# Two mixer layers move from the Gelu activation to a GELU built from Tanh, with a new plan for the schedule

## The chip, the cores and the metric

The kernel runs on one core of a Trainium2 chip. The metric is the device time of one execution in microseconds (us). Six runs of the kernel before lie between 1075.77 and 1081.0 us, with a median of 1077.77 us. In this text PE is the matrix engine (TensorE), ACT the activation engine (ScalarE), DVE the vector engine (VectorE), POOL is GpSimd and SP is the engine that issues most DMAs.

## What is computed

Two layers, each an attention block and a mixer block, on x of shape 1 x 2048 x 448 in bf16. Cut to what matters:

```python
def _A_ref(x, wqkv, wo):            # attention, 16 heads of 28
    q, k, v = split(x @ wqkv)
    p = softmax(q @ k.T * 28 ** -0.5)
    return (p @ v) @ wo
def _B_ref(x, w1, w2, w3, w4):      # mixer, F = 1792
    h = gelu_tanh(layernorm(x) @ w1)
    hs = shift_quarters_by(-1, +1, -2, +2)(h) @ w2
    x1 = x + hs
    return x1 + gelu_tanh(layernorm(x1) @ w3) @ w4
for _ in range(2):
    x = x + _A_ref(layernorm(x), wqkv, wo)
    x = x + _B_ref(layernorm(x), w1, w2, w3, w4)
```

The GELU is the one with tanh: gelu(x) = x/2 * (1 + tanh(sqrt(2/pi) * (x + 0.044715 x^3))). "The wide GELU" below is the one of the last line, on 1792 features of a token.

## The kernel before

**Tiles and work.** The 2048 tokens are 16 tiles of 128. Attention goes over query chunks of each layer: tiles 0-3, 4-7, 8-11, 12-13 and 14-15. For a chunk and a group of four heads (a "segment") the scores of one key tile and one head are a block of 128 keys x 512 (chunk and keys so arranged that a block is always 512 wide); there are 1024 blocks per layer. PE makes the scores (line 1292), ACT takes the exponential of three or two blocks at a time out of PSUM into the tile `PT` (line 1447), and PE multiplies with v (line 753). A few blocks do not go to ACT: the planner may give a block to DVE, which computes its exponential in five instructions (lines 1333, 1354, 1356, 1358, 1361, through the tiles `yd`, `fb` and `PD`). How many of a segment may go that way is bounded by the table `D_RATE` for (layer, chunk); a further condition is that the plan shows PE idle there and that buffers are free.

**The mixer.** When a chunk's attention is done, the output projection (lines 762, 1606) and the first mixer half `t_mixA` follow. Its GELU is already built from Tanh (`t_tanh`): DVE halves the matmul's result into `hT` (line 1676), POOL squares it into a buffer of `fb` (1694), DVE does one scalar_tensor_tensor (1695), ACT the Tanh in place (1696), DVE a second scalar_tensor_tensor (1697). `fb` has three buffers of 512 floats a partition; the DVE exponentials and the attention's normalisation (line 1548) take buffers from the same three.

The second half `t_mixB` works on groups of tiles 0-2, 3-6, 7-10, 11-12 and 13-15 of each layer. A group's 14 products with `w3`, each 128 features x 256, 384 or 512 tokens, are cast by DVE from PSUM to the bf16 tile `h2T` (line 1813, operation CAST). When all 14 are there, ACT applies one `Gelu_apprx_tanh` over all of them in place (line 1822: 128 x 7168 for four tiles, 5376 for three, 3584 for two), and PE multiplies with `w4` (line 762, `ps<-w,h2T`). Work after the last exponential does it directly from PSUM (line 1809, and lines with PT or vaug as output). Exponential and Tanh use one activation table, this Gelu another, so that a Gelu between exponentials brings two ACT_TABLE_LOADs, one ahead of it (listed under line 1822) and one ahead of the next exponential (line 1447).

**What sets the order.** Nothing is issued dynamically. When the program is built, a list scheduler (`Sched`) runs generators, one per piece of work, against durations written in the code, and fixes the order of the instructions on each engine; at run time each engine goes through its own list in order and waits on semaphores. If two pieces are ready at once, the lower rank goes first. Ranks come from `RANK` (a and b: the two mixer halves of a chunk, k and q: projections of keys and queries), `Q_LEAD` says how many segments ahead the queries of a chunk are loaded, `PE_NORM` where the normalisation is done by PE. On ACT the instruction that is ready first goes first. PE keeps two PSUM banks for everything but scores and the product with v (`misc`); it fills planned gaps with matmuls on `ident` (line 1863), which compute nothing that is used.

Of the kernel before, what the change touches and what calls it, by code (L numbers as in the profile page):

```python
# [513 lines left out]
DLO = 5  # L514
DHI = 7
DPK = 2
RANK = {k: round(1.1 + 0.05 * i, 3) for i, k in enumerate([('b', 0, 0), ('a', 0, 0), ('k', 0, 1), ('b', 0, 1), ('k', 0, 2), ('k', 1, 0), ('q', 0, 2), ('q', 0, 1), ('k', 1, 2), ('a', 0, 1), ('k', 1, 1), ('q', 0, 3), ('q', 1, 0), ('b', 0, 3), ('k', 0, 3), ('q', 1, 1), ('a', 0, 2), ('b', 0, 4), ('b', 0, 2), ('a', 0, 3), ('a', 0, 4), ('k', 1, 4), ('b', 1, 0), ('a', 1, 0), ('a', 1, 3), ('k', 1, 3), ('a', 1, 4), ('a', 1, 2), ('a', 1, 1), ('b', 1, 4), ('q', 1, 2), ('b', 1, 3), ('q', 1, 3), ('b', 1, 2), ('b', 1, 1)])}
Q_LEAD = {(0, 1): 6, (0, 2): 9, (0, 3): 3, (1, 0): 7, (1, 1): 9, (1, 2): 4, (1, 3): 5}
D_RATE = {(0, 0): 0.08, (0, 1): 0.05, (0, 2): 0.05, (0, 3): 0.06, (1, 0): 0.16, (1, 1): 0.1, (1, 2): 0.16}
PE_NORM = {(0, 0): False, (0, 1): False, (0, 2): False, (0, 3): False, (0, 4): False, (1, 0): False, (1, 1): False, (1, 2): False, (1, 3): False, (1, 4): True}  # L520
Sched.AGED = 0.1
Sched.TARGET = 0.64
Sched.LOW = 0
# [21 lines left out]
def build_kernel(nc, A_x, A_wqkv, A_wo, B_x, B_w1, B_w2, B_w3, B_w4, out, n_layers=2):  # L545
# [78 lines left out]
    with st:  # L624
# [97 lines left out]
        def num1(r):  # L722
            return int(r[1:])
# [4 lines left out]
        def op(eng, dur, fn, reads=(), writes=(), **kw):  # L728
            return (eng, dur, fn, list(reads), list(writes), kw)
# [36 lines left out]
        def later(ops, bank=None, sigs=()):  # L766
            for o in ops:
                yield o
            if bank is not None:
                yield ("rel", bank)  # L770
            for g_ in sigs:
                yield ("sig", g_)
# [913 lines left out]
                if t % HR == 0 and t > 0:  # L1686
                    yield ("spawn", t_halo(L, t), 2)

        def t_tanh(L, t0, grp, z, NW, hk):
            yield ("wait", ("hz", L, t0, grp))  # L1690
            fr = yield ("acq", FB, hk)
            fk = ("fb", num1(fr))
            f = fb[0:112, num1(fr), 0:NW]
            yield op("pool", 0.2 + NW * 0.00165, lambda e: e.tensor_tensor(out=f, in0=z, in1=z, op=ALU.mult), reads=hk, writes=[fk])  # L1694
            yield op("dve", 0.05 + NW * 0.00108, lambda e: e.scalar_tensor_tensor(out=f, in0=f, scalar=0.25 / GK, in1=z, op0=ALU.add, op1=ALU.mult), reads=hk + [fk], writes=[fk])
            yield op("act", c_act(NW), lambda e: e.activation(out=f, in_=f, func=ACT.Tanh, scale=8.0 * GK * (2.0 / math.pi) ** 0.5), reads=[fk], writes=[fk], tab="exp")  # L1696
            yield op("dve", 0.05 + NW * 0.00108, lambda e: e.scalar_tensor_tensor(out=z, in0=f, scalar=1.0, in1=z, op0=ALU.add, op1=ALU.mult), reads=hk + [fk], writes=hk)
            yield ("rel", fr)
            yield ("sig", ("hA", L, t0, grp))

        def t_halo(L, t):
            yield ("wait", ("mixA", L, t - 1))
# [69 lines left out]
        def t_mixB(L, tiles, direct, pr):  # L1772
# [25 lines left out]
            else:  # L1798
                yield ("acq", [hname], [("xT", xt)])
                hb, hkey = h2T, [[("h2T", f), ("xst",)] for f in range(14)]  # L1800
            late = []
            for fch in range(14):
                b = yield misc(("xT", xt))
                for fc in FCS:
                    yield op("pe", c_mm(NW), (mm4 if NW > 300 else mm)(ps[:, bi(b), 0:NW], w3[:, fc, 128 * fch:128 * fch + 128], xv(xt)[:, fc, 0:NW], fc == 0, fc == 3),
                             reads=[("xT", xt), ("w3",)], writes=[("ps", bi(b))], touch=[b], mode="col4" if NW > 300 else "plain")
                hk = hkey[fch]
                if direct or ("tail",) in SC.events:
                    ev = op("act", c_act(NW), lambda e, fch=fch, b=b: e.activation(out=hb[:, fch, 0:NW], in_=ps[:, bi(b), 0:NW], func=ACT.Gelu_apprx_tanh),
                             reads=[("ps", bi(b))], writes=hk, touch=[b], tab="gelu")  # L1810
                else:
                    late.append(fch)
                    ev = op("dve", c_ps(NW), lambda e, fch=fch, b=b: e.tensor_copy(out=hb[:, fch, 0:NW], in_=ps[:, bi(b), 0:NW]),  # L1813
                            reads=[("ps", bi(b))], writes=hk, touch=[b])
                yield ("spawn", later([ev], b, [("h2", L, tiles[0], fch)]), 1.5)
            yield ("rel", x_)
            for fch in range(14) if not direct else ():
                yield ("wait", ("h2", L, tiles[0], fch))
            if late:
                nl = len(late)  # L1820
# [3 lines left out]
            for i, t in enumerate(tiles):  # L1824
# [2 lines left out]
                b = yield misc(hkey[late[-1] if late else 0][0])  # L1827
                yield ("wait", ("xx1", L, t))
                for fch in range(14):
                    if direct:  # L1830
                        yield ("wait", ("h2", L, tiles[0], fch))
                    yield op("pe", c_mm(D) + 0.0, mm4(ps[:, bi(b), 0:D], hb[:, fch, 128 * i:128 * i + 128], w4[:, fch, :], fch == 0, fch == 13),
                             reads=[hkey[fch][0], ("w4",)], writes=[("ps", bi(b))], touch=[b], mode="col4", slack=slack if fch == 0 else 0.0)
                if L == 0:
# [126 lines left out]
```

## Time and profile before

| what | value |
|---|---|
| median of six runs | 1077.77 us |
| the execution that was profiled | 1080.7 us |
| its span, first to last instruction | 1079.0 us |
| granted TensorE clock, mean | 0.992 |
| ACT exponentials (line 1447) | 805, busy 921.9 us |
| blocks exponentiated on DVE (line 1333) | 37 |
| wide Gelus in one piece (line 1822) | 8, busy with their table loads 41.9 + 10.3 us |
| Tanh instructions (line 1696) | 36 |
| table loads | 16: one at the start, 8 ahead of a Gelu, 7 ahead of an exponential |
| last exponential's successor starts at | 1024.54 us |

The eight wide Gelus start, in us of the span, at 236.48, 376.69, 520.32, 609.20 and 653.92 (layer one) and at 840.95, 915.26 and 1025.83 (layer two). Their widths name the tile groups: the one at 609.20 is the only 3584-wide one, tiles 11-12 of layer one; the one at 915.26 is 7168 wide, tiles 3-6 of layer two. The page gives busy time as a union, so that instructions which overlap on one engine count once; the mean duration of one instruction includes the overlap with its neighbour.

### The profile page before, as it was taken

How to read it: one execution, taken by the hardware profiler on the slowest of the kernel's cores; microseconds unless marked ns; L12 is line 12 of the kernel's file. 1: busy time of each engine (PE TensorE's matmuls, PEld its weight loads, DVE VectorE, ACT ScalarE, POOL GpSimd, SP SyncE). 2: the span in 40 equal slices, each digit the busy share in tenths (PEclk: the TensorE clock that was granted, in tenths of full speed). 3: DMA queues.
4: the chain of work that ended last, by engine and by line, in shares of the span. 5: the costliest groups of instructions: out<-in, count | busy, mean ns of one | idle time of the engine just before them, and what ended most of it. 6: DMA issues, size and time to landing. Idle time of an engine off the chain costs nothing.

```text
span 1079.0 us, 35127 instructions
## 1 busy us (share of the span) xinstructions
PE 1009.4 (94%) x15921; PEld 421.1 (39%) x15921; DVE 637.2 (59%) x1234; ACT 1018.0 (94%) x919; POOL 313.1 (29%) x506
## 2 busy tenths in 40 slices
PE   6999999999999999899999999999989999999998
PEld 2333443443333344344433333353333433443465
DVE  8777669946569525766256553524796394554551
ACT  6898999999999999999999999999999999999951
POOL 2244124401254014452042201102743030432130
PEclk9999999999999999999999999999999999999999
DMA  4647221003111022120121133413411110220000
GB/s 114 138 112 211 76 56 32 23 17 91 32 32 32 12 69 66 44 42 20 38 81 45 26 97 98 132 53 105 84 27 27 42 40 12 53 58 16 12 11 32
DMA packets 92613, 62.24 MB, mean 58 GB/s; under 512 B 64688, under 2 KB 82368, under 8 KB 92464
## 3 DMA queue, kind: packets, MB, share of 16 engines
q1 hardware_dynamic: 89088, 51.92, 18.6%
q0 software_dynamic: 3376, 8.09, 2.7%
q8 instruction: 124, 2.03, 0.8%
q14 instruction: 25, 0.20, 0.1%
HBM read 27.12 MB, written 15.71 MB: 40 GB/s over the span
## 4 chain that ended last, share of the span: by engine, by line
ACT 70%; PE 18%; DVE 7%; DMA 2%; issue 1%; SPq 1%; POOL 1%; DVEq 0%
ACT PT L1447 63%; PE ps L762 10%; PE ps L1292 4%; ACT h2T L1822 4%; PE ps L753 3%; ACT fb L1696 1%; ACT L1822 1%; DVE fb L1356 1%; PE ps L1863 1%; DMA rT<-ub 1%; DVE PD L1361 1%; ACT L1447 1%; DVE rT L1541 1%; DVE yd L1333 1%; DVE fb L1354 1%
## 5 line engine op out<-in xcount | busy, mean ns | idle before, releaser
L1447 ACT ACTIVATE PT<-ps 128x1536 bf16<-128x1536 f32 (+1 forms) x805 | 921.9, 1335 | 20.0 <-PE ps L1292 19.2
L1292 PE MATMUL ps<-qT,kT 32*128 32x512 bf16 (+1 forms) x2560 | 315.6, 341 | 31.7 <-ACT PT L1447 23.4
L753 PE MATMUL ps<-PT,vaug 128*32 128x512 bf16 (+1 forms) x2523 | 252.3, 342 | 0.0
L1292 PEld LDWEIGHTS ps<-qT,kT 32*128 32x128 bf16 x2560 | 80.7, 91 | 309.2 <-ACT PT L1447 278.7
L1863 PE MATMUL ps<-ident 128*32 128x256 bf16 x3688 | 166.1, 275 | 3.7 <-POOL ident L842 1.5
L762 PE MATMUL ps<-xT,w 128*32 128x512 bf16 (+2 forms) x1600 | 127.7, 360 | 2.8 <-DVE h2T L1813 1.9
L1863 PEld LDWEIGHTS ps<-ident 128*32 128x32 bf16 x3688 | 105.2, 97 | 31.6 <-issue 12.1
L1813 DVE CAST h2T<-ps 128x512 bf16<-128x512 f32 (+2 forms) x112 | 67.9, 606 | 80.5 <-PE ps L762 73.1
L762 PE MATMUL ps<-w,h2T 128*32 128x448 bf16 x1512 | 104.8, 365 | 10.2 <-ACT h2T L1822 9.8
L753 PEld LDWEIGHTS ps<-PT,vaug 128*32 128x32 bf16 x2523 | 74.6, 95 | 94.9 <-issue 81.6
L1552 POOL TENSOR_TENSOR otn<-ub,fb 128x512 bf16<-128x512 f32 (+1 forms) x36 | 40.4, 1121 | 174.5 <-DMA fb<-rscr 174.5
L1088 POOL TENSOR_TENSOR sq<-kT 128x512 bf16<-128x512 bf16 (+2 forms) x32 | 30.0, 941 | 121.2 <-DVE kT L1102 120.6
L1694 POOL TENSOR_TENSOR fb<-hT 112x512 f32<-112x512 bf16 (+1 forms) x36 | 37.7, 1049 | 82.9 <-DVE hT L1676 73.5
L762 PEld LDWEIGHTS ps<-w,h2T 128*32 128x32 bf16 x1512 | 42.2, 98 | 47.0 <-issue 18.2
L762 PEld LDWEIGHTS ps<-xT,w 128*32 128x32 bf16 (+1 forms) x1600 | 44.1, 95 | 42.0 <-issue 19.3
L1768 POOL TENSOR_TENSOR x_res<-x_res,x1b 128x448 f32<-128x448 f32 x32 | 40.3, 1263 | 23.9 <-DVE xn L959 23.8
L1333 DVE TENSOR_SCALAR yd<-ps 128x512 int32<-128x512 f32 x37 | 24.9, 679 | 34.4 <-PE ps L1292 34.1
L1541 DVE RECIPROCAL rT<-rT 16x128 f32<-16x128 f32 (+1 forms) x36 | 33.5, 932 | 17.9 <-DMA rT<-ub 17.9
L1822 ACT ACTIVATE h2T<-h2T 128x7168 bf16<-128x7168 bf16 (+2 forms) x8 | 41.9, 5244 | 0.1
L762 PE MATMUL ps<-kT,w 128*32 128x512 bf16 (+1 forms) x576 | 40.1, 360 | 1.9 <-DVE qT L1164 1.1
L1526 DVE COPY ub<-ps 128x512 f32<-128x512 f32 (+1 forms) x40 | 23.3, 583 | 30.7 <-PE ps L753 30.1
L762 PE MATMUL ps<-xT,wq_pad 128*32 128x512 bf16 x448 | 41.0, 405 | 0.3 <-DVE qT L1135 0.2
(164 smaller groups left out, 1168.4 us busy)
## 6 DMA issues: line engine op xcount, KB each, us to landing
uscr<-ub SPq DMA_DIRECT2D x24, 256.0 KB, 2.0
ub<-uscr SPq DMA_DIRECT2D x24, 256.0 KB
fb<-rscr SPq DMA_DIRECT2D x24, 256.0 KB
xnd<-xn SPq DMA_DIRECT2D x28, 128.0 KB, 2.0
x_res<-in_A_x_dram POOLq DMA_DIRECT2D x16, 224.0 KB, 4.2
xd<-x_res SPq DMA_DIRECT2D x16, 224.0 KB, 2.2
x_res<-xd SPq DMA_DIRECT2D x16, 224.0 KB, 4.2
out_dram<-obf SPq DMA_DIRECT2D x16, 112.0 KB
```

The lines of the kernel that those rows point to most:

```text
L753: return lambda e: e.matmul(out=out, lhsT=lhsT, rhs=rhs, start=start, stop=stop, **kw)
L762: r.append(e.matmul(out=out[c:c + w, :], lhsT=lhsT[:, c:c + w], rhs=rhs, start=start, stop=stop, tile_position=(0, c)))
L1292: yield op("pe", max(0.055, 0.22 / nc_ * NW / 512.0), lambda e, i=i, kc=kc, j=j, g=g, a=a, NW=NW, bank=bank: e.matmul(out=ps[:, bank, i * ...
L1333: yield op("dve", c_ps(512), lambda e: e.tensor_scalar(out=y, in0=ps[:, bi(bank), :], scalar1=SCALE * L2E * FS, scalar2=-126.0 * FS, op0=A ...
L1447: yield op("act", 0.06 + n * w * 0.000833, lambda e, bk=bk, s0=s0, n=n, w=w: e.activation(out=PT[:, s0:s0 + n, 0:w], in_=ps[:, bk[0]:bk[0] ...
L1541: yield op("dve", 0.86, lambda e: e.reciprocal(out=rT[0:4 * n, :], in_=rT[0:4 * n, :]), reads=[("rT",)], writes=[("rT",)])
L1552: yield op("pool", 0.2 + NW * 0.0021, lambda e: e.tensor_tensor(out=otn[:, g, 0:NW], in0=u, in1=rb[:, 0:NW], op=ALU.mult), reads=[uk, fk], ...
L1694: yield op("pool", 0.2 + NW * 0.00165, lambda e: e.tensor_tensor(out=f, in0=z, in1=z, op=ALU.mult), reads=hk, writes=[fk])
L1768: yield op("pool", 1.2, lambda e: e.tensor_tensor(out=X, in0=X, in1=X1, op=ALU.add), reads=[xk, ("x1b", s)], writes=[xk], deps=[nop_])
L1813: ev = op("dve", c_ps(NW), lambda e, fch=fch, b=b: e.tensor_copy(out=hb[:, fch, 0:NW], in_=ps[:, bi(b), 0:NW]), reads=[("ps", bi(b))], wri ...
L1822: yield op("act", c_act(nl * NW), lambda e: e.activation(out=hb[:, 0:nl, 0:NW], in_=hb[:, 0:nl, 0:NW], func=ACT.Gelu_apprx_tanh), reads=al ...
L1863: return [e.matmul(out=ps[32 * c:32 * c + 32, bi(b), 0:256].rearrange("p (a n) -> p a n", n=128), lhsT=ident[:, 32 * c:32 * c + 32], rhs=i ...
```

## The change

The tile groups 11-12 of layer one and 3-6 of layer two no longer use the one Gelu. For them the step from PSUM to `h2T` multiplies by 0.5, and a new generator does the five-step GELU of `t_tanh` in place on 512 columns at a time: one of the 14 feature blocks for four tiles, two of them for two tiles. That makes 14 pieces for tiles 3-6 and 7 for tiles 11-12. The matmuls with `w4` wait for each feature block's piece instead of for the one Gelu. `t_tanh` itself is only rewritten to use the shared function. `RANK`, `Q_LEAD` and `D_RATE` get new values (22 of the 35 keys of RANK change their place, by one to five places; the queries of tiles 8-11 of layer two rise by four; D_RATE of layer two falls from 0.16 to 0.03 for tiles 0-3 and from 0.16 to 0.1 for tiles 8-11).

```diff
-RANK = {... [('b',0,0),('a',0,0),('k',0,1),('b',0,1),('k',0,2),('k',1,0),('q',0,2),('q',0,1),('k',1,2),... ('k',1,4),('b',1,0),('a',1,0),('a',1,3),('k',1,3),('a',1,4),('a',1,2),('a',1,1),('b',1,4),('q',1,2),('b',1,3),('q',1,3),('b',1,2),('b',1,1)]}
-Q_LEAD = {(0, 1): 6, (0, 2): 9, (0, 3): 3, (1, 0): 7, (1, 1): 9, (1, 2): 4, (1, 3): 5}
-D_RATE = {(0, 0): 0.08, (0, 1): 0.05, (0, 2): 0.05, (0, 3): 0.06, (1, 0): 0.16, (1, 1): 0.1, (1, 2): 0.16}
+RANK = {... [('a',0,0),('b',0,0),('k',0,1),('k',0,2),('k',1,0),('k',1,2),('q',0,2),('b',0,1),('q',0,1),... ('b',0,2),('a',1,0),('a',1,3),('a',1,2),('q',1,2),('k',1,3),('a',1,4),('a',1,1),('b',1,4),('b',1,3),('q',1,3),('b',1,2),('b',1,1)]}
+Q_LEAD = {(0, 1): 4, (0, 2): 9, (0, 3): 3, (1, 0): 7, (1, 1): 10, (1, 2): 4, (1, 3): 5}
+D_RATE = {(0, 0): 0.08, (0, 1): 0.05, (0, 2): 0.05, (0, 3): 0.06, (1, 0): 0.03, (1, 1): 0.1, (1, 2): 0.1}
+TANHW = {(0, 0): 0, (0, 3): 0, (0, 7): 0, (0, 11): 1, (0, 13): 0, (1, 0): 0, (1, 3): 1, (1, 7): 0, (1, 11): 0}
...
+        def tanh_gelu(z, rows, NW, hk, view):
             fr = yield ("acq", FB, hk)
             fk = ("fb", num1(fr))
+            f = view(fb[0:rows, num1(fr), 0:NW])
             yield op("pool", ..., lambda e: e.tensor_tensor(out=f, in0=z, in1=z, op=ALU.mult), ...)
             yield op("dve", ..., lambda e: e.scalar_tensor_tensor(out=f, in0=f, scalar=0.25 / GK, in1=z, op0=ALU.add, op1=ALU.mult), ...)
             yield op("act", ..., lambda e: e.activation(out=f, in_=f, func=ACT.Tanh, scale=8.0 * GK * (2.0 / math.pi) ** 0.5), ..., tab="exp")
             yield op("dve", ..., lambda e: e.scalar_tensor_tensor(out=z, in0=f, scalar=1.0, in1=z, op0=ALU.add, op1=ALU.mult), ...)
             yield ("rel", fr)
+        def t_tanh_w(L, t0, fs, hb, NW, hk):
+            for fch in fs:
+                yield ("wait", ("h2", L, t0, fch))
+            z = hb[:, fs[0]:fs[-1] + 1, 0:NW]
+            yield from tanh_gelu(z, 128, NW * len(fs), hk, lambda f: f.rearrange("p (a n) -> p a n", n=NW))
+            for fch in fs:
+                yield ("sig", ("h2g", L, t0, fch))
...
+            soft = TANHW.get((L, tiles[0]), 0) and not direct
+            fps = 512 // NW
...
+                if soft:
+                    ev = op("dve", c_ps(NW), lambda e, fch=fch, b=b: e.tensor_scalar(out=hb[:, fch, 0:NW], in0=ps[:, bi(b), 0:NW], scalar1=0.5, scalar2=None, op0=ALU.mult), ...)
+                elif direct or ("tail",) in SC.events:
...
+                if soft and (fch % fps == fps - 1 or fch == 13):
...
+                    yield ("spawn", t_tanh_w(L, tiles[0], fs, hb, NW, hks), pr)
...
-            for fch in range(14) if not direct else ():
+            for fch in range(14) if not direct and not soft else ():
                 yield ("wait", ("h2", L, tiles[0], fch))
...
-                    if direct:
-                        yield ("wait", ("h2", L, tiles[0], fch))
+                    if direct or soft:
+                        yield ("wait", ("h2g" if soft else "h2", L, tiles[0], fch))
```

## Prediction

> **What bounds the kernel now.** I read the busy shares first, then the chain of work that ended last, then the activation groups with shapes kept apart, the waits, and last the two places where the Gelus stand in the timeline. The page, in order: busy time of ACT, the 40 slices of ACT, the chain by engine.
>
> ```profile
> PE 1009.4 (94%) x15921; PEld 421.1 (39%) x15921; DVE 637.2 (59%) x1234; ACT 1018.0 (94%) x919; POOL 313.1 (29%) x506
> ...
> ACT  6898999999999999999999999999999999999951
> ...
> ACT 70%; PE 18%; DVE 7%; DMA 2%; issue 1%; SPq 1%; POOL 1%; DVEq 0%
> ```
>
> ACT is full from the third slice to the 38th; only the last 50 us (slices 39 and 40) have it idle. PE's 94% is less than it seems, since 166 us of it are the filler matmuls of line 1863. ACT waits little: in the waits of ACT the exponentials stand still 19.2 us in 15 places, nearly always for scores:
>
> ```profile
> ACT PT L1447 <- PE ps L1292: 19.2, 15, 4.0
> ```
>
> In the timeline 9.4 us of these fall before 88 us (1.89, 3.96, 3.58); the rest are a dozen of 0.3 to 2.4 us. So up to the last exponential (1024.5 us) the time is the sum of what ACT does plus those stalls, and a microsecond taken from ACT there is worth one. After it come 54.5 us in which PE has matmuls back to back; ACT is no bound there.
>
> The two Gelus that the change touches, as ACT's timeline shows them (start, duration):
>
> ```profile
> 606.87 1.02 ACT L1447 ACTIVATE PT<-ps 128x1024 bf16<-128x1024 f32 x1
> 607.90 1.28 ACT L1822 ACT_TABLE_LOAD   x1
> 609.20 3.19 ACT L1822 ACTIVATE h2T<-h2T 128x3584 bf16<-128x3584 bf16 x1
> 612.40 1.28 ACT L1447 ACT_TABLE_LOAD   x1
> 613.70 1.45 ACT L1447 ACTIVATE PT<-ps 128x1536 bf16<-128x1536 f32 x1
> ```
>
> ```profile
> 913.97 1.28 ACT L1822 ACT_TABLE_LOAD   x1
> 915.26 6.18 ACT L1822 ACTIVATE h2T<-h2T 128x7168 bf16<-128x7168 bf16 x1
> 921.46 1.28 ACT L1447 ACT_TABLE_LOAD   x1
> 922.75 2.37 ACT L1447 ACTIVATE PT<-ps 128x1024 bf16<-128x1024 f32 x2
> ```
>
> And two Tanhs of the first mixer half between exponentials: no table load, and the next instruction starts 0.52 us after the Tanh, though its own duration reads 0.63 to 0.67.
>
> ```profile
> 776.63 0.63 ACT L1696 ACTIVATE fb<-fb 112x512 f32<-112x512 f32 x1
> 777.15 4.62 ACT L1447 ACTIVATE PT<-ps 128x1536 bf16<-128x1536 f32 x4
> 781.62 0.67 ACT L1696 ACTIVATE fb<-fb 112x512 f32<-112x512 f32 x1
> 782.14 1.49 ACT L1447 ACTIVATE PT<-ps 128x1536 bf16<-128x1536 f32 x1
> ```
>
> **ACT, removed.** From the first load to the next exponential: 613.70 - 607.90 = 5.80 us and 922.75 - 913.97 = 8.78 us, together 14.58. Ahead of a load the exponential before must drain. The groups of line 1447 sum to 622.0 + 452.2 + 0.8 = 1075.0 us against 921.9 busy, so neighbours overlap by 153.1 / 805 = 0.19 us, lost once at each place: 0.38. Removed: 14.96 us.
>
> **ACT, added.** 14 pieces for tiles 3-6 and 7 for tiles 11-12, each 512 columns. The rows above give 0.52 us each in line (112 or 128 partitions are worked in parallel): 21 x 0.52 = 10.92. If every one stood alone it would be the mean duration of the 512-wide form, 0.71: 14.9. Net: 14.96 - 10.92 = **-4.0 us** (0.0 if all stand alone).
>
> [...]
>
> **DVE and POOL, added.** The cast becomes a scaling with the same shapes: 0.689 (line 1813) against 0.685 us (line 1676), nothing. Each piece adds two scalar_tensor_tensors (lines 1695 and 1697: median 0.68, mean 0.83) and one POOL multiply (median 1.04). For tiles 11-12 that is 14 x 0.68 = 9.5 us of DVE and 7.3 of POOL around 590 to 612, where DVE is 6 to 7 tenths busy: hidden. For tiles 3-6 it is 28 x 0.68 = 19.0 us of DVE and 14.6 of POOL. There DVE, in stretches of 10 us, reads:
>
> ```profile
> 860.00:870.00 10.00, 6.56 (x13) 1.00 0.19 49
> 870.00:880.00 10.00, 9.70 (x16) 1.00 0.21 43
> 880.00:890.00 10.00, 9.86 (x17) 1.00 0.08 28
> 890.00:900.00 10.00, 5.96 (x10) 1.00 0.01 2
> 900.00:910.00 10.00, 3.97 (x6) 1.00 0.08 29
> 910.00:920.00 10.00, 6.09 (x13) 1.00 0.02 5
> ```
>
> The sum is 42.1 of 60 us, idle 17.9: the added 19.0 fill it, at the mean of 0.83 (23.2) overfill it by 5.4. The casts lie at 883 to 913, so most of the pieces fall in the later, emptier rows and can run past 920. I count it as hidden; what it costs uncovered is the slow rival.
>
> Latency: the first Tanh of the run starts on POOL at 183.1 and its second scalar_tensor_tensor ends at 188.1, so a piece needs 5.0 us and holds one of three `fb` buffers: 14 pieces need at least 14 / 3 x 5.0 = 23.3 us, less than the 29 us in which the casts come. The last piece ends 5.0 us after the last cast (912.7), so `w4` can start near 917.7 instead of 921.5; nothing on the path gains by it directly. The wait on each piece stands on PE ahead of the `w4` matmuls; scores queue behind it in PE's order. And the first `w4` product may take one of two free PSUM banks a few us before the last piece is done. Planned right this costs nothing; the case that it isn't is in the rivals.
>
> GpSimd's multiply meets DVE's two-input instructions: in the trace a scalar_tensor_tensor of line 1356 lasts 1.52 us at 877.99 beside a POOL add from 877.43 to 878.95, against its median of 0.685. [...]
>
> **DVE exponentials.** A block on DVE takes 921.9 / 2011 = 0.458 us from ACT (2011 = 3 x 402 + 2 x 402 + 1 blocks on ACT) and costs DVE 0.68 + 0.76 + 0.83 + 0.44 + 0.71 = 3.4 us. Of the 37, ten lie in layer two's tiles 8-11 (785 to 887 us), five of them in the segment from 869 on; one lies at 616.6 in its tiles 0-3. With 0.03 that last chunk still allows 0.03 x 4 x 7 = 0.84, so one a segment: nothing need go. With 0.1 the sixth key block allows 2.4 where 0.16 allowed 3.84, so three taken instead of four. I take two blocks lost: **+0.9 us**. Bounds: three gained elsewhere (-1.4), all ten lost (+4.6).
>
> **The new order.** No row shows it. The stall it most plainly touches is that of ACT at 743.84 (2.37 us) and its echo at 772.01 (0.85): a query projection of layer two was evacuated late, because DVE's list had a reciprocal ahead of it that waited 3.21 us for a DMA (at 739.59). The queries of tiles 8-11 rise four ranks. Both stalls gone is -3.2; a like pair new is +3.2. I take **-1.0**, nearer to nothing. The stalls before 88 us hang on the first key and value projections, whose ranks among each other hardly change: 0.
>
> **The tail.** Tiles 7-10's last cast (1023.12) ends just before the last exponential. Were it earlier, their Gelu would go among the exponentials: 6.18 + 2 x 1.28 + 0.19 = 8.9 us more for ACT, against 10.9 us of `w4` matmuls (224) taken out of the tail: -2.0. Were the casts to stay where they are while ACT ends 4 us sooner, ACT would wait, but those matmuls are PE's last work (from 1065), 33 us after the Gelu's end, so it is covered; +2.6 without that cover. I take 0.
>
> **Sum.** -4.0 + 0.9 - 1.0 + 0 = -4.1 us: 1080.7 - 4.1 = 1076.6 for the profiled execution. That one was 2.9 us above the median of six, so on the median 1077.77 - 4.1 = **1073.7 us**.
>
> **Rivals.**
> *More is gained* (0.25): the seam stalls go, no DVE block is lost, the tail swap comes: -4.0 - 3.2 - 2.0 = -9.2, 1068.6. For it: ACT is the bound everywhere and every term is there in the rows; against it, they must all fall right.
> *Nothing is left* (0.10): the change does remove four loads but its room on DVE is paid with five DVE blocks (+2.3) and one stall of about 1: -0.7, 1077.1. For it: D_RATE falls just where the pieces go.
> *Slower* (0.23): DVE becomes the bound around tiles 3-6. Already before, the chain runs through DVE from 870.85 to 886.8 and ACT loses 0.68 there. With 5.4 us of excess passed on to the scores through late casts and query evacuations, and one more seam like 743.84: -4.0 + 0.9 + 5.4 + 2.4 = +4.7, 1082.4. It decides from the point where ACT stands still 7.2 us longer than before. Against it: DVE is 59% busy over the span, and DVE blocks can give way.
> *The forecast* (0.42): 1072 to 1075.5.
>
> **Numbers.** A measurement of this kernel can tell about 0.3%, 3.2 us, from no change: below 1074.5 counts as faster, above 1081.0 as slower. Of the forecast 0.32 lies below 1074.5 and 0.10 above. Faster: 0.32 + 0.25 = 0.57. Same: 0.10 + 0.10 = 0.20. Slower: 0.23. The range takes in most of both rivals, 1068 to 1083, and leaves about 0.1 out on each side.
>
> **What would show it.** Right: 12 table loads instead of 16, six wide Gelus, 57 Tanhs, ACT's busy time some 3 us less, 35 or so DVE blocks, the last exponential done about 4 us sooner with a tail still near 54 us. Wrong: ACT's wait for scores well above 19.2 us, above all after 860 us; DVE full for 30 us on end there; far fewer than 35 blocks; or a tail of other length, which would mean that the order, not the tables, made the difference.

## The result, and the profile after

The kernel after the change takes 1084.16 us in the median of its 16 timed runs, the kernel before 1078.12 us (37 runs): a ratio of **1.0055, 95% interval 1.0043 to 1.0067**. The change makes the kernel slower by 6 us where 4 us less were forecast. The execution that was profiled took 1084.23 us, with a span of 1082.5 us and a mean granted TensorE clock of 0.992.

Lines of the kernel after are those of before plus one from line 753 on (1292 becomes 1293, 1447 becomes 1448), the Gelu is line 1845, the cast 1830, the new scaling 1823, the fillers 1886; 1694 to 1697 (the pieces of the Tanh GELU) keep their numbers.

The page of the kernel after: busy time by engine, then ACT's 40 slices.

```profile
PE 1002.3 (93%) x15701; PEld 414.8 (38%) x15701; DVE 664.4 (61%) x1273; ACT 1015.6 (94%) x937; POOL 345.1 (32%) x527
...
ACT  6898999999999999999999999999998989999952
```

ACT does 2.4 us less than before and the span is still 3.5 us longer. The new thing is in the slices: an 8 stands at 31 and at 33, where before there were nines from the fifth slice to the 38th. A slice is 27 us, so the place is 812 to 893 us. The waits of ACT (engine, line, what it waited for; total, times, longest) tell the same:

```profile
ACT PT L1448 <- PE ps L1293: 21.0, 20, 4.0
...
ACT fb L1696 <- DVE fb L1695: 3.4, 3, 1.5
```

The exponentials wait 1.8 us longer than before, and Tanhs now make ACT wait 3.4 us, before 0.1: ACT takes its list in order, so a Tanh whose DVE step is late holds up the exponentials behind it (1.52 us at 887.37, below).

What the tables promised is there: 12 table loads, 6 wide Gelus, 57 Tanhs. All 37 DVE blocks are still there. To see where the time went I cut the stream of exponentials at the same number of finished blocks in both traces, and split ACT's time of each stage (from the start of one instruction to the start of the next, in us, idle time apart):

| blocks done | before: length, idle | after: length, idle | difference |
|---|---|---|---|
| 0 to 1000 | 512.0, 20.4 | 508.5, 17.5 | -3.5 |
| 1000 to 1250 (tiles 11-12 of layer one) | 131.3, 1.2 | 128.6, 0.8 | -2.7 |
| 1250 to 1500 | 123.2, 2.4 | 122.3, 1.6 | -0.9 |
| 1500 to 1750 (766 to 895 us) | 127.9, 2.4 | 135.7, 8.8 | +7.8 |
| 1750 to 1875 (tiles 3-6 of layer two) | 67.2, 0.1 | 70.2, 3.9 | +3.0 |
| 1875 to 2011 | 62.9, 0.0 | 62.8, 0.1 | -0.2 |
| tail after the last exponential | 54.45 | 54.43 | 0.0 |

So the change is 7 us ahead at 760 us and has lost 10.8 us by 965. Of the 7 the 2.7 of tiles 11-12 are its own. The 3.5 of the first 1000 blocks, where only the order differs, are mostly chance of one execution: the profiled run of before had four stretches of half clock before 530 us (see the last section), that of after none, and three kernels below that have the tables of before (e1, e1b, v4) need 509.1 to 510.3 us for these blocks. Over the whole stream Gelus lose 9.4, table loads 5.1, Tanhs add 11.3 and idle time adds 6.2.

The prediction showed DVE in stretches of 10 us from 860. After the change the same view reads (length, DVE busy, instructions, granted clock, DMA):

```profile
860.00:870.00 10.00, 8.19 (x16) 1.00 0.27 63
870.00:880.00 10.00, 9.79 (x16) 1.00 0.22 56
880.00:890.00 10.00, 9.86 (x14) 0.83 0.01 2
890.00:900.00 10.00, 8.81 (x12) 1.00 0.01 2
900.00:910.00 10.00, 8.06 (x13) 1.00 0.02 3
910.00:920.00 10.00, 7.11 (x12) 1.00 0.08 28
```

DVE is busy 51.8 of 60 us where it was 42.1. It is full from 870 to 890 in both kernels; after the change the 20 us behind that are fuller too, 8.8 and 8.1 instead of 6.0 and 4.0. But it is not a matter of totals: from 880 to 890 it runs 14 instructions where before it ran 17 in the same 9.86 us. They last longer. The timeline of the kernel after at that place (start, duration, engine, line, operation, idle time before it and what ended that):

```profile
881.77 1.42 POOL L1694 TENSOR_TENSOR fb<-h2T 128x512 f32<-128x512 bf16 x1 [5.28 <-DVE h2T L1823]
...
882.21 1.53 DVE L1355 SCALAR_TENSOR_TENSOR fb<-yd 128x512 f32<-128x512 uint16 x1
...
883.15 1.71 POOL L1553 TENSOR_TENSOR otn<-ub,fb 128x512 bf16<-128x512 f32 x1
...
883.77 1.64 DVE L1357 SCALAR_TENSOR_TENSOR fb<-fb,yd 128x512 f32<-128x512 f32 x1
885.33 0.68 DVE L1334 TENSOR_SCALAR yd<-ps 128x512 int32<-128x512 f32 x1
...
886.07 0.40 PE L763 MATMUL ps<-xT,w 128*32 128x512 bf16 x4 [2.03 <-DVE yd L1334]
...
886.64 0.69 DVE L1695 SCALAR_TENSOR_TENSOR fb<-fb,h2T 128x512 f32<-128x512 f32 x1
...
887.37 0.63 ACT L1696 ACTIVATE fb<-fb 128x512 f32<-128x512 f32 x1 [1.52 <-DVE fb L1695]
...
887.71 2.28 PE L763 MATMUL ps<-xT,w 128*32 128x512 bf16 x16
...
890.36 2.37 ACT L1448 ACTIVATE PT<-ps 128x1536 bf16<-128x1536 f32 x2 [1.45 <-PE ps L1293]
```

Read it downwards. A wide square starts on POOL at 881.77 and ends at 883.19; a two-input DVE instruction that starts at 882.21 ends at 883.74, 0.55 us later. The next POOL instruction ends at 884.86, the next DVE instruction at 885.41, again 0.55 later. Both took 1.5 to 1.6 us instead of 0.68. DVE's evacuation of a PSUM bank (line 1334) comes late, PE waits 2.03 us for it, the scores behind in PE's order come late; DVE's step for a Tanh (1695) comes late too, and ACT stands 1.52 us before the Tanh and 1.45 us before the next exponential. And the 16 matmuls at 887.71 take 2.28 us, because the granted clock is 0.50 for 3.41 us after PE's wait.

### The profile page after: what moved, and what is told of

It reads as the page before. It is cut to its first block, busy times and chain, and to the rows that moved or that the text cites. A ratio compares the mean times of both kernels' runs of the same rounds, so it can differ in the third digit from the quotient of the medians.

```text
span 1082.5 us, 34808 instructions
## 1 busy us (share of the span) xinstructions
PE 1002.3 (93%) x15701; PEld 414.8 (38%) x15701; DVE 664.4 (61%) x1273; ACT 1015.6 (94%) x937; POOL 345.1 (32%) x527
## 3 DMA queue, kind: packets, MB, share of 16 engines
q8 instruction: 123, 2.02, 0.8%
## 5 line engine op out<-in xcount | busy, mean ns | idle before, releaser
L1886 PE MATMUL ps<-ident 128*32 128x256 bf16 x3468 | 154.8, 274 | 3.2 <-POOL ident L843 1.5
L1886 PEld LDWEIGHTS ps<-ident 128*32 128x32 bf16 x3468 | 98.1, 96 | 29.6 <-issue 11.2
L1830 DVE CAST h2T<-ps 128x384 bf16<-128x384 f32 (+1 forms) x81 | 50.2, 619 | 58.1 <-PE ps L763 57.5
L1694 POOL TENSOR_TENSOR fb<-hT 112x512 f32<-112x512 bf16 (+1 forms) x36 | 38.7, 1079 | 65.2 <-DVE hT L1677 54.0
L763 PE MATMUL ps<-xT,wk_pad 128*32 128x512 bf16 (+2 forms) x576 | 46.8, 365 | 0.2 <-DVE kT L1103 0.2
L946 POOL TENSOR_SCALAR vpe<-mv 128x1 f32<-128x1 f32 (+2 forms) x21 | 5.7, 271 | 114.0 <-DVE mv L941 114.0
L1694 POOL TENSOR_TENSOR fb<-h2T 128x512 f32<-128x512 bf16 x21 | 28.2, 1349 | 42.4 <-DVE h2T L1823 21.5
L763 PE MATMUL ps<-wv,xT 128*32 128x448 bf16 x512 | 41.0, 360 | 0.6 <-DVE vaug L1181 0.6
```

The costliest lines, as they stand in the source:

```text
L763: r.append(e.matmul(out=out[c:c + w, :], lhsT=lhsT[:, c:c + w], rhs=rhs, start=start, stop=stop, tile_position=(0, c)))
L1886: return [e.matmul(out=ps[32 * c:32 * c + 32, bi(b), 0:256].rearrange("p (a n) -> p a n", n=128), lhsT=ident[:, 32 * c:32 * c + 32], rhs=i ...
```

## The theories

*POOL's squares*: the 21 wide squares meet DVE's two-input instructions in a stretch where DVE is full; that is the larger part of the loss. *DVE's load*: the 42 wide scalar_tensor_tensors by themselves are too much for DVE there, whoever runs beside it. *The plan*: the new tables cost by themselves, wherever Tanh is put.

## Experiments: the parts of the change

Each ratio is to the kernel before, run on the same chip. "No wide Tanh" is the kernel after with all of `TANHW` at 0.

```diff
-TANHW = {..., (0, 11): 1, ..., (1, 3): 1, ...}
+TANHW = {..., (0, 11): 0, ..., (1, 3): 0, ...}   # e2: no wide Tanh, new tables
+TANHW = {..., (0, 11): 1, ..., (1, 3): 0, ...}   # e3: tiles 11-12 alone, new tables
+TANHW = {..., (0, 11): 0, ..., (1, 3): 1, ...}   # e4: tiles 3-6 alone, new tables
 # e1: both, with RANK, Q_LEAD and D_RATE of before; e1b: tiles 11-12 alone, with those
```

> The tables of before (RANK, Q_LEAD, D_RATE) with Tanh in both wide groups. Three theories. Pieces: the 14 pieces of tiles 3-6 of layer two overfill DVE and POOL around 880 to 950 us, whatever the order; then this is slower than before, about 1083 us. Order: the new tables are what costs, the pieces alone would save the 4 us worked out; then this is about 1074. Clock: each half-clock stretch of PE (3.4 us long) costs about 3 us, and time follows their number; then time = that of before - 4 + 3 x (stretches more than the five of before).

> The new tables with no wide Tanh: eight Gelus as before. Pieces: about that of before, 1078 us, perhaps a little less since the new tables gained 3 to 4 us up to 600 us. Order: slower, about 1086 to 1088 (the 1084 of the changed kernel plus the 4 us that the tables of ACT save).

> The changed kernel with the one Gelu back for tiles 3-6 of layer two; only tiles 11-12 of layer one keep Tanh. Pieces: the stalls of 880 to 960 us go, about 1074 to 1076 us. Order: they stay or move, 1083 to 1086.

> The changed kernel with the one Gelu back for tiles 11-12 of layer one; only tiles 3-6 of layer two keep Tanh. Pieces: as slow as the changed kernel plus the 2.3 us that tiles 11-12 saved, 1086 us, with ACT idle again 6 to 7 us between 880 and 960. Order: the same time, but then the third kernel of this set is slow as well.

> The tables of before, Tanh in tiles 11-12 of layer one alone. If the pieces of tiles 3-6 and the new tables are the two losses, this has neither and keeps the 2.3 us of tables and Gelu that tiles 11-12 save: 2 us faster than before. If any new order brings its own stalls, it comes out anywhere within 5 us.

| kernel | ratio to before, 95% interval |
|---|---|
| after | 1.0055 [1.0043, 1.0067] |
| e2, new tables, no wide Tanh | 1.0030 [1.0012, 1.0049] |
| e3, new tables, tiles 11-12 | 1.0018 [1.0000, 1.0036] |
| e4, new tables, tiles 3-6 | 1.0045 [1.0030, 1.0060] |
| e1, tables of before, both | 1.0105 [1.0083, 1.0126] |
| e1b, tables of before, tiles 11-12 | 1.0058 [1.0035, 1.0082] |

With the new tables the medians say: plan +3.2 us, tiles 11-12 -1.3 (e2 to e3) or +1.1 (e4 to after), tiles 3-6 +1.6 (e2 to e4) or +4.0 (e3 to after). The intervals of neighbours overlap, so the single parts are estimates; that tiles 3-6 are the losing half is what m1 below bears out. With the tables of before both pieces cost 11 us: the parts do not add up across plans. Some expectations missed: e1 is slower than any of its three theories had it (1090 us), e3 does not have the 2 to 4 us that the theory of the pieces gave it, and e1b was to be 2 us faster, or anywhere within 5, and is 6.3 slower. One of the twelve executions of e4 took 2921.69 us and is not in its ratio.

e1b went another way. There the casts of tiles 7-10 of layer two come early enough for their Gelu to go ahead of the last exponential: the tail is 49.1 us, 5.4 less, but the last exponential ends at 1037.6, 13.1 us later than before, of which the Gelu and its two loads are 8.75 and four blocks that DVE no longer takes (33 instead of 37) 4 x 0.458 = 1.8. The prediction had given this swap -2.0.

What the plan costs in e2 is not one stall. From 600 us on ACT stands still 9.5 us in e2's profile and 4.5 in that of before. The longest stall of e2 is at a seam:

```profile
765.66 0.94 DVE L1542 RECIPROCAL rT<-rT 16x128 f32<-16x128 f32 x1 [3.93 <-DMA rT<-ub]
...
767.25 1.47 PE L763 MATMUL ps<-xT,w 128*32 128x512 bf16 x12 [1.93 <-DVE qT L1165]
...
769.31 2.48 ACT L1448 ACTIVATE PT<-ps 128x1536 bf16<-128x1536 f32 x2 [2.49 <-PE ps L1293]
```

DVE's list has a reciprocal that waits 3.93 us for a DMA, the evacuation of a query projection stands behind it, PE waits 1.93 us for that, ACT 2.49 us for scores. It is the mechanism that the prediction had read at 743.84 in the kernel before, at another seam, and there it was nearly as long (2.37 us). So this stall took the place of the one before; the difference is in shorter ones, 1.16 us at 740, 1.9 from 885 to 892 and 2.2 from 991 to 996, whose causes stay open.

## Experiments: the same order with one cost taken out

In m1 and m2 the order is that of the kernel after, since the durations that the planner reckons with are unchanged; only the instruction's real size differs. m4 and c4, further down, are planned anew.

```diff
+            c1 = (lambda v: v[..., 0:1] if len(v.shape) == 3 else v[:, 0:1]) if rows == 128 else (lambda v: v)
-            ... e.tensor_tensor(out=f, in0=z, in1=z, op=ALU.mult)                      # m1: POOL's square
+            ... e.tensor_tensor(out=c1(f), in0=c1(z), in1=c1(z), op=ALU.mult)
-            ... e.scalar_tensor_tensor(out=f, in0=f, scalar=0.25 / GK, in1=z, ...)      # m2: both DVE steps
+            ... e.scalar_tensor_tensor(out=c1(f), in0=c1(f), scalar=0.25 / GK, in1=c1(z), ...)
```

> The changed kernel with every instruction in the same order, but the 21 POOL squares of the wide pieces do one column of each feature block instead of all (the rest of the square is left out, so the GELU of those two groups is not computed). What remains is what DVE and the order cost. If POOL and its meeting with DVE's two-input instructions is the cause of the stalls from 880 us on, ACT's idle time from 865 to 965 us falls from some 7 us to about 2, and the time to about 1079 us; if DVE's own load is the cause, little changes (1083 us).

> The same with the 42 scalar_tensor_tensors of the wide pieces cut to one column instead (left out: the rest of both). If DVE's load is the cause, the stalls from 880 us on go and the time falls to about 1079 us; the stalls at 765 to 820 us, which have another cause, stay. If POOL is the cause: about 1082 us.

m1: **1.0005 [0.9986, 1.0024]**. m2: **1.0040 [1.0023, 1.0058]**. Taking POOL's squares out gives back 5.0 thousandths, 5.4 us; cutting twice as many DVE instructions gives back 1.5, and there the intervals overlap. m1's timeline at the place shown above:

```profile
881.38 0.57 POOL L1695 TENSOR_TENSOR fb<-h2T 128x1 f32<-128x1 bf16 x1 [5.27 <-DVE h2T L1824]
...
881.82 0.68 DVE L1355 SCALAR_TENSOR_TENSOR fb<-yd 128x512 f32<-128x512 uint16 x1
881.91 1.72 POOL L1553 TENSOR_TENSOR otn<-ub,fb 128x512 bf16<-128x512 f32 x1
...
882.53 1.64 DVE L1357 SCALAR_TENSOR_TENSOR fb<-fb,yd 128x512 f32<-128x512 f32 x1
...
884.83 0.40 PE L763 MATMUL ps<-xT,w 128*32 128x512 bf16 x4 [1.19 <-DVE yd L1334]
...
885.91 1.25 PE L763 MATMUL ps<-xT,w 128*32 128x512 bf16 x16
...
886.13 0.63 ACT L1697 ACTIVATE fb<-fb 128x512 f32<-128x512 f32 x1 [0.68 <-DVE fb L1696]
```

The square is short, the first DVE instruction takes 0.68 us again, the second still meets POOL's other instruction (1.72, ended by 883.63; DVE ends 0.54 later). PE waits 1.19 us instead of 2.03, ACT 0.68 instead of 1.52 and not at all afterwards, and the same 16 matmuls take 1.25 us instead of 2.28: no half clock. In the stage of tiles 3-6 ACT's idle time falls from 3.9 to 0.0 us and its length from 70.2 to 65.2, now 2.0 less than before: about the gain that the tables promised for these tiles. All 42 DVE steps are there at full length, so DVE's load by itself is not what stalls ACT. In the stage ahead of it 6.8 of 8.8 us idle remain, the longest 2.0 us at 766 and 2.2 at 817; e2 has the first of these (2.49) and 0.56 near the second.

m2's profile is that of its slowest run (1084.99 us). In it the stage of tiles 3-6 is 65.0 us long with 0.0 us idle, as in m1: there it is enough to take either side of the meeting away. What m2 leaves is the pair of stalls ahead of that stage:

```profile
893.16 0.63 ACT L1697 ACTIVATE fb<-fb 128x512 f32<-128x512 f32 x1 [0.99 <-DVE fb L1696]
...
896.59 6.21 ACT L1448 ACTIVATE PT<-ps 128x1536 bf16<-128x1536 f32 x5 [1.76 <-PE ps L1293]
```

They are 2.75 us against 1.52 + 1.45 in the kernel after and 0.68 in m1. There the squares meet DVE's exponentials, which m2 leaves as they are. From 765 to 827 us ACT stands 9.4 us in m2's profile and 5.6 in that of the kernel after, though the two have the same order there and nothing cut: one profile of each does not tell why.

m1 does not part two ways in which a square can hold DVE. One is the meeting. The other is plain waiting for the square to end, as here in the kernel after:

```profile
912.20 0.69 DVE L1823 TENSOR_SCALAR h2T<-ps 128x512 bf16<-128x512 f32 x1 [1.03 <-POOL fb L1694]
...
937.73 1.51 DVE L1695 SCALAR_TENSOR_TENSOR fb<-fb,h2T 128x512 f32<-128x512 f32 x1 [2.13 <-POOL fb L1694]
```

From 860 to 965 us DVE waits 4.7 us for squares in this way, 1.5 in m1 and 0.3 in before. m1 shortens the square itself (mean 1.35 to 0.50 us) and so takes from both; v1, further down, does too. That the squares cost these 5 us is shown; how it divides between meeting and waiting is not.

```diff
-D_RATE = {..., (1, 2): 0.1}
+D_RATE = {..., (1, 2): 0.0}     # m4: no exponentials on DVE in tiles 8-11 of layer two
```

> The changed kernel with D_RATE of layer two's tiles 8-11 at 0: no exponential on DVE between 765 and 895 us. ACT takes them: ten blocks more are 4.6 us. If the meeting of DVE exponentials and wide pieces is what stalls ACT around 885 us, some 3 to 4 us come back and the time stays within 2 us of the changed kernel, with DVE no longer full from 870 to 900 us; if not, it is 4 to 5 us slower.

m4: 1.0026 [1.0010, 1.0043], with 27 DVE blocks. ACT takes ten blocks more, 10 x 0.458 = 4.6 us, and the kernel is still 3 us faster than after (by the medians' ratios). Idle time in the two stages is 4.6 and 0.4 us against 8.8 and 3.9. That fits a price for the meeting of DVE's exponentials with the squares, but it is a new plan, whose seams differ too, and it does not tell POOL from DVE, since it takes DVE's side of the meeting away.

```diff
-yield op("pool", 0.2 + NW * 0.00165, ...)
+yield op("pool", (1.6 if rows == 128 else 0.2 + NW * 0.00165), ...)   # c4
```

> The changed kernel, but the planner reckons 1.6 us for each of the 21 wide POOL squares instead of 1.045 (they took 1.35 in the mean). The plan is made anew with it. If the loss around 880 to 955 us comes from a plan that trusts a POOL that is faster than the real one, ACT's waits for the wide pieces (3.4 us) fall below 1 us and the time by 2 to 3 us, to 1081. If any plan of these pieces meets the same contention, it stays at 1083 to 1086.

c4: 1.0100 [1.0070, 1.0130]. The planner now knows a square's price of 1.6 us, makes a new plan, and is worse: stalls of 4.5, 2.8 and 2.7 us at 692, 741 and 771, a tail of 58.1. Both expected times (1081, or 1083 to 1086) were missed. The planner's price was too low (it reckons 1.045; the median in the trace is 1.42), but a truer price did not make a better plan.

## Experiments: is it the clock?

```diff
-    ... ps[32 * c:32 * c + 32, bi(b), 0:256] ... rhs=ident[...].to_broadcast([128, 2, 128])
+    ... ps[32 * c:32 * c + 32, bi(b), 0:512] ... rhs=ident[...].to_broadcast([128, 4, 128])   # f1: after, f2: before
```

> The changed kernel with every instruction in the same order; only the filler matmuls of PE, whose result nobody uses, stream 512 columns instead of 256. If PE's half-clock stretches are a cause of lost time and not only its mark, they get fewer: granted clock from 0.991 to 0.995 or more, and the time falls by some 0.87 us for each 0.001, to about 1080 us. If they are only a mark of stalls that come from elsewhere, the time stays at 1084, or grows because the fillers stand in PE's way.

> The kernel before with the same wider fillers, order unchanged. By the clock as cause: granted clock from 0.995 to 0.998, time down by 2 to 3 us to about 1075. By the clock as a mark: no change or slower.

f1: 1.0479 [1.0453, 1.0505]; f2: 1.0468 [1.0443, 1.0493]. Fillers of double length hold the clock up (profiled at 0.998 and 1.000, without them 0.992 in both) but stand in PE's way: the kernel before loses 50 us by them, the kernel after 46. The two come out 0.1% apart, which hints that clock is part of the difference; with 50 us of another stall in both it settles nothing.

## Experiments: the squares moved off POOL, and the tables one by one

```diff
+            wd = rows == 128                                    # v1: wide squares on DVE, in bf16
-            f = view(fb[0:rows, num1(fr), 0:NW])
+            f = view(fb[0:rows, num1(fr), :].bitcast(BF16)[:, 0:NW] if wd else fb[0:rows, num1(fr), 0:NW])
-            yield op("pool", 0.2 + NW * 0.00165, ...)
+            yield op("dve" if wd else "pool", 0.45 if wd else 0.2 + NW * 0.00165, ...)
 # s1: no wide Tanh, D_RATE of before; s2: no wide Tanh, RANK and Q_LEAD of before
 # v2: v1 with RANK and Q_LEAD of before; v3: v1 with D_RATE of before; v4: v1 with all three
```

> The kernel with no wide Tanh at all, with the changed RANK and Q_LEAD and the D_RATE of before. With all three tables changed and no wide Tanh the time was 1.0030 of before, 3.2 us more; stalls stood at 769 us, where PE waited 1.9 us for a query evacuation. Theory A (the new ranks put DVE's reciprocal, which waits for a DMA, in the way of that evacuation): nearly all of it is here, 1.002 to 1.004, with the stall of about 2.5 us at 765 to 772. Theory B (the lower D_RATE moves DVE blocks to worse places): 1.000 here. Theory C (no one table; each new plan throws the stalls anew): a number that neither half explains, with the largest stall at another place.

> The kernel with no wide Tanh, with the RANK and Q_LEAD of before and the changed D_RATE alone. Theory A (ranks): 1.000. Theory B (D_RATE): 1.002 to 1.004. Theory C (every new plan throws the stalls anew): this and the run with the ranks alone do not add up to the 1.0030 of both together; either of them may be above it.

> The kernel after, planned anew, with the 21 wide squares taken from POOL to DVE, and the square and Tanh argument kept in bf16 instead of f32 (all the rest of the arithmetic as after). Theory A (POOL's wide squares and their meeting with DVE's two-input instructions cost about 5 us, as the run with the squares cut to one column showed): the scalar_tensor_tensors stay near 0.69 us, and with about 21 x 0.4 = 8 us more on DVE the time falls to 1.000 to 1.003 of before. Theory B (DVE is the bound in that stretch, whoever stretches it): 1.005 or more, with DVE full from 870 to 910 us. Either is blurred by the plan, which is new.

> The kernel with the wide squares on DVE in bf16 (0.9992 of before, its last exponential 2.9 us earlier than before's, its tail 1.7 us longer, one pair of stalls of 2.8 and 1.8 us at 737 to 741 left), with the RANK and Q_LEAD of before. The ranks alone, with no wide Tanh, cost 2.1 to 2.9 us. Theory A (the ranks' cost adds to the pieces' gain): 0.996 to 0.998. Theory C (each new plan throws the stalls at the seams anew, by some 3 us either way): anything from 0.996 to 1.003, and the seam near 740 to 770 decides.

> The kernel with the wide squares on DVE in bf16, with the D_RATE of before and the changed RANK and Q_LEAD. Theory A (D_RATE alone costs next to nothing, 0.7 us without wide Tanh): 0.999. If DVE's own load were the bound at tiles 3-6 (theory B), the larger D_RATE there, which allows more DVE blocks, would cost: 1.002 or more. Theory C: 0.996 to 1.003, by the seam.

> The kernel with the wide squares on DVE in bf16 and all three tables as before. With the squares on POOL and these tables it was 1.0105. Theory A (POOL's squares are what costs): 0.996 to 1.000. Theory C (the plan's seams): may lie anywhere up to 1.010, with the loss then at the same place as in that run, between 640 and 900 us, and not at tiles 3-6.

| kernel | tables | ratio, 95% interval | last exponential ends | tail |
|---|---|---|---|---|
| s1, no wide Tanh | D_RATE of before | 1.0027 [1.0007, 1.0047] | 1024.0 | 55.2 |
| s2, no wide Tanh | RANK, Q_LEAD of before | 1.0007 [0.9991, 1.0022] | 1025.5 | 54.5 |
| v1, squares on DVE | new | 0.9992 [0.9974, 1.0009] | 1021.6 | 56.2 |
| v2, squares on DVE | RANK, Q_LEAD of before | 1.0012 [0.9992, 1.0031] | 1021.8 | 57.7 |
| v3, squares on DVE | D_RATE of before | 0.9993 [0.9969, 1.0017] | 1022.6 | 56.2 |
| v4, squares on DVE | all of before | 1.0031 [0.9999, 1.0062] | 1022.4 | 57.7 |

v1 puts 21 more instructions on the engine that was said to be full, and the loss is gone. Its plan has 34 DVE blocks instead of 37, so its load of DVE is not that of the kernel after plus the squares. The squares take 0.42 us there (bf16 in and out), and the stage of tiles 3-6 is 64.5 us long with 0.05 us idle. Its stretches of 10 us there read (PE, weight loads, DVE, ACT and POOL busy, then clock and DMA):

```profile
880.00:890.00 10.00, 8.81 (x115) 2.75 (x119) 9.51 (x15) 9.06 (x9) 1.58 (x1) 1.00 0.02 6
890.00:900.00 10.00, 10.00 (x145) 3.29 (x145) 8.18 (x14) 9.95 (x11) 0.00 (x0) 1.00 0.01 2
900.00:910.00 10.00, 8.74 (x182) 4.45 (x176) 8.81 (x16) 10.00 (x12) 0.00 (x0) 1.00 0.03 7
910.00:920.00 10.00, 8.45 (x170) 4.45 (x170) 8.83 (x14) 10.00 (x13) 1.27 (x1) 1.00 0.07 27
```

DVE is as full as in the kernel after (8.2 to 9.5 of 10) and ACT is full beside it. So the theory of DVE's load falls, and that of POOL's squares holds, in two ways (m1 and v1); v1 has a plan of its own, m1 has not. v4 against e1, the same tables without and with squares on POOL, points the same way: 1.0031 against 1.0105. But v4 lies above the 0.996 to 1.000 that were expected if POOL's squares were all.

For the tables, ranks cost 2.9 us and the rate 0.7 us with no wide Tanh (the interval of the rate includes no change), which nearly adds up to the 3.2 of both. But setting the ranks back in v1 did not give 2 us (v2: +2.2 us by the medians' ratios, intervals overlapping). In the profiles the seam stall moves: at 737 to 741 us in v1 (2.81 and 1.77, after a reciprocal that waited 7.52 us for its DMA), at 765 to 771 in s2 and e2, at both in s1, at neither in v2. The ranks' price belongs to one plan and is no term that can be added.

No version beats the kernel before by more than can be told. In v1 and v2 the last exponential ends 2.9 and 2.7 us earlier than before, about what the ACT sum allows, and the tail gives 1.7 and 3.2 us of it back. PE's groups in the tail show one thing that slipped there, products of tiles 7-10 with `w3`; before has no such line in its tail. In v1, in v2, and in the kernel after:

```profile
L763 PE MATMUL ps<-xT,w 128*32 128x512 bf16 x40 | 3.0, 381 | 0.0
```

```profile
L763 PE MATMUL ps<-kT,w 128*32 128x512 bf16 x100 | 5.8, 379 | 0.0
```

```profile
L763 PE MATMUL ps<-xT,w 128*32 128x512 bf16 x36 | 2.7, 380 | 0.0
```

The kernel after has nearly as many of them as v1 and yet a tail of 54.43 us, so they do not explain v1's longer tail. v2 has 3.1 us more of them than the kernel after, and its tail is 3.2 us longer. What sets the length of the tail stays open: m1's last exponential ends 4.3 us earlier than before's, and its tail is 54.0.

## Why the prediction was wrong, step by step

*ACT, removed and added (-14.96 + 10.92 = -4.0): right but for 0.8 us.* Measured over the stream: Gelus -9.4, loads -5.1, Tanhs +11.3, net -3.2. A Tanh costs 11.3 / 21 = 0.54 us in line, 0.52 was read.

*DVE exponentials (+0.9): wrong by that much.* None was lost.

*DVE and POOL, added: this is the step that failed.* The prediction said "I count it as hidden". It had the row that speaks against it: a two-input DVE instruction of 1.52 us beside a POOL add. It weighed it by totals, idle 17.9 us against 19.0 added, and set it to nothing. Measured: m1 gets 5.4 us back by cutting POOL's part alone. The total of the stretching is small. In the kernel before 22 two-input DVE instructions are stretched, by 16.4 us together; after, 30, by 21.7. From 860 to 950 us the counts are 5 and 10, by 3.2 and 7.1 us. Five more meetings are 4 us of DVE, and waiting for squares is another 4.4 (4.7 against 0.3, from 860 to 965). They fall where DVE has little slack and PE and ACT stand behind it in order; the timelines above show that for the stalls at 887 and 890, and for the others it is argued. The prediction also read its latency too short: the last piece was to end 5.0 us after the last cast, and it ends at 950.7, 36 us after the last scaling (914.3). And it reckoned the pieces with POOL's 1.04 us; a wide square's median is 1.42:

```profile
L1694 POOL TENSOR_TENSOR fb<-hT x36: 613/1041/1954, 181.9 to 1010.2; 112x512 f32<-112x512 bf16 x24, 112x256 f32<-112x256 bf16 x12
...
L1694 POOL TENSOR_TENSOR fb<-h2T x21: 1040/1422/2212, 572.9 to 937.7; 128x512 f32<-128x512 bf16 x21
```

8 more two-input DVE instructions are stretched than before, by 5.3 us more in all; behind a wide square end five of the 30, and e2, with no wide Tanh at all, has 24.

*The new order (-1.0): wrong in sign.* e2 measures +3.2 us (interval 1.3 to 5.3) for the tables alone. The bounds of 3.2 either way just held, the choice inside them did not. The stall that it named did leave 743.84, and one of the same kind and length came at 769; the cost is in shorter ones.

*The tail (0): right for the kernel after* (54.43 against 54.45). The swap, priced at -2.0, was seen in e1b and loses: 8.75 us of ACT, as read, but the tail gave 5.4 for it and not 10.9.

*The slow rival* had the place (tiles 3-6), the sign and nearly the time (1082.4), with DVE as the bound. What decides is not DVE's added load but POOL in its way, and about half of the loss is the plan's. Its turning point was 7.2 us more standstill of ACT; over the whole stream it is 6.2 more, from 766 us on 10.4 (12.8 against 2.4).

*The sum with the measured terms:* -3.2 (ACT) + 0 (DVE blocks) + 5.4 (m1) + 3.2 (e2) + 0 (tail) = +5.4 us, where 6.0 were measured. The terms come from different runs, with intervals of about 2 us, so that they fit within 0.6 us may be luck.

*Not in the sum at all: the clock.* See the last section.

## What to carry to other kernels

Work that is moved to POOL and DVE is not free because their idle time adds up (here 17.9 us idle for 19.0 added, and m1 gets 5.4 back): look at the stretch where it lands, count which DVE instructions with two SBUF inputs would run beside it, reckon with their ending after the POOL instruction (the 30 stretched ones here end 0.5 to 0.6 us after it) and not after their own 0.68 us, and count what DVE's list waits for on POOL (4.7 us here from 860 to 965). When an engine's list is fixed, a late evacuation is paid by what stands behind it in order (here PE 2.03 us, then ACT 1.52 and 1.45); price the chain DVE, PE, ACT and not the DVE time alone. A new plan's own seams can be worth as much as a change of this size (e2: 3.2 us, against 3.2 taken from ACT): run the new plan without the change before crediting either.

## What the runs showed of the hardware that was not expected

**POOL and DVE hold each other up.** In the rows above, a DVE scalar_tensor_tensor that starts while a POOL tensor_tensor runs ends 0.54 to 0.56 us after it: 883.19 to 883.74, 884.86 to 885.41, in m1 883.63 to 884.17, and in the kernel before (877.43 + 1.52 = 878.95 to 879.51). Over the kernel after 30 two-input DVE instructions are stretched over 0.85 us, and all 30 end 0.5 to 0.6 us after the POOL instruction beside them; in before 21 of 22. This looks like a wait for the whole instruction, not a slower pace. It goes the other way too: of the 21 wide squares the 11 that start while such a DVE instruction runs take 1.42 to 1.55 us, as at 894.48, and 9 others 1.04, as at 901.09. Some cases do not fit: at 208.40, 209.01, 772.50 and 905.15 a two-input DVE step takes 0.62 to 0.68 us inside a POOL instruction of 1.95 to 2.79 us (the last inside a square of 2.21 from 904.46), and two that start inside POOL's one-column instructions of line 1638, at 172.35 and 174.16, take 0.68 us. Two kinds that read PSUM are not stretched. All 37 of line 1334, with one input, from PSUM, take 0.62 to 0.69 us, the one at 778.15 inside a POOL instruction from 777.72 to 778.99 too. All 32 of line 1607, with one of two inputs from PSUM, take 0.55 to 0.62 us, the one at 917.19 beside a square that ends at 917.68 too. Line 1359, with one input from SBUF, mostly takes 0.42 us, but 1.15 at 893.25 beside a square that runs from 892.69 to 894.11; why, no run here tests.

**PE's clock halves for 3.41 us at a time, also after a stretch in which PE was partly busy.** The kernel after, all engines, in the four windows of about that length around 886.4 (columns as above; clock third from the end):

```profile
879.50:882.90 3.40, 3.16 (x40) 0.85 (x36) 3.37 (x6) 3.39 (x4) 1.12 (x1) 1.00 0.06 22
882.90:886.40 3.50, 0.99 (x14) 0.32 (x14) 3.47 (x4) 2.95 (x3) 1.96 (x2) 1.00 0.00 0
886.40:889.80 3.40, 3.40 (x30) 0.70 (x19) 3.33 (x6) 1.54 (x2) 1.55 (x1) 0.50 0.00 0
889.80:893.20 3.40, 3.40 (x45) 1.07 (x44) 2.62 (x5) 2.83 (x3) 0.51 (x1) 1.00 0.00 0
```

PE was busy for 0.99 of 3.5 us, and in the next window it ran at half clock. The longest wait of a matmul there was 2.03 us. Before has five such stretches in its profiled span, after has five stretches' length in four places, all after 780 us; m1 loses the one at 886.

The length of a wait does not decide. PE waits 2.02 us near 380 and 2.20 near 522 us in both kernels; in before the clock halves after each (from 383.15 and 526.51), in after it does not. Within one run the stretches start on a grid whose step is their own length, 3.413 us: those of before, at 154.46, 383.15, 458.24, 526.51 and 741.55, lie 67, 22, 20 and 63 such steps apart (587.09 us in 172 steps), those of after, at 780.60, 814.74, 886.42 and 941.03, 10, 21 and 16 (160.43 us in 47). So where a wait falls on the grid may be what differs between two executions. How busy PE must be in a step is not shown: in before 0.69 of the step ahead of 154.46 was busy and the clock halved, in after 0.42 of the step ahead of 524.6 and it did not.

The mean granted clock of a run goes closely with its time: 17 runs of the kernel after go from 1078.43 us at 0.997 to 1089.09 at 0.987 (correlation -0.88), and over the runs of e1 to e4, m1, m2, m4, c4 and before, each against its kernel's mean, a thousandth of clock goes with about 0.9 us. One stretch is 3.41 x 0.5 / 1082 = 0.0016, so by that an estimated 1.4 us, where the clock theory of e1 took about 3. The mean clock is 0.9909 after against 0.9941 to 0.9958 for before in the five sets of runs: some 3 to 4 of the 6 us go along with more such stretches, as part of the terms above and not beside them. That is a correlation; a wait lengthens the run and lowers the clock at once, and f1 and f2, which were to part the two, did not.
